# Three plain fp32 steps in the first half batch in place of eight, with a planner that counts table loads and transfer issue

## The chip, the cores and the metric

The kernel runs on one core of one Trainium2 chip. The metric is device time of one execution in microseconds (us). A core has five engines that run their own instruction streams in order: TensorE (PE in the profile; its weight loads are listed apart as PEld), VectorE (DVE), ScalarE (ACT), GpSimd (POOL) and SyncE (SP), which here issues all transfers. Inputs and outputs are fp32.

## The reference

Sliding-window attention with pooled keys and values, followed by a gated feed-forward layer, for 4 batches of 768 positions, 8 heads of 64, model width 512 and inner width 1024. Cut to what is computed:

```
block, window = 32, 16
k_sum = k in blocks of 32, max;  v_sum = v in blocks of 32, mean
scores = [ scale * q @ k^T where |i - j| < 16, else -1e9 ;  scale * q @ k_sum^T + log(32) ]
a = softmax(scores);  x = a @ [v ; v_sum]          # (B, 768, 512)
xk = mu_k * x + (1 - mu_k) * x_prev                # x_prev: x shifted by one position
xr = mu_r * x + (1 - mu_r) * x_prev
k = max(xk @ w_k, 0);  v = (k * k) @ w_v
r = 1 / (1 + exp(-(xr @ w_r)))
out = r * v
```

## The kernel before

A batch is cut into two halves of 384 positions; the eight halves are called by batch and half (b, hf). The attention of one half and one pair of heads is a *unit*: 24 small score products (L441), six masked copies with a running minimum on VectorE (L452), six exponentials on ScalarE (L456), sums and reciprocals on VectorE (L462, L463), six scalings on GpSimd (L468, tile `y`), two groups of three transposes on TensorE (L475, tile `pt`), their copies on ScalarE (L479), 24 value products (L488, tile `av`) and a copy of the result. A half has four units, so there are 32.

The feed-forward layer of a half begins with `mix` (L510 to L524), which forms xr and xk per pair of heads. From the second half on, each is then split into a high fp32r part (`cast` on ScalarE) and the low rest (`sub` on VectorE, L524). Three *gate tiles* give xr @ w_r, each followed by a sigmoid (L533) into a `z` tile. Then come eight *steps* j = 0 to 7: a *first product* xk @ w_k for 128 inner columns (L580), relu and square on ScalarE (L587, L589), a split of the square into `kh` and `kl` (L593 to L595), and a *second product* with w_v (L606) that accumulates over the eight steps into three PSUM tiles. After step 7, VectorE multiplies these with `z` (L636, the *results*), and they are stored. PSUM has four tiles called `mm` (mm_132 to mm_135 in the order's rows): the gates, the first products and the three accumulators share them.

A product is made in one of two ways. In the split way it takes three fp32r products, high by high, high by low and low by high: 12 matmuls in a first product, 9 in a second. In the plain way (`single`) it is one fp32 product with unsplit operands: 4 and 3 matmuls, each of which stands as two records in the trace. In half (0, 0), before the change, all eight steps and the gate are plain. The weights come as 64-bit words; ScalarE and VectorE turn each into fp32 (L307, L310, L312), and a split into high and low (L324 or L325, L327) follows for all 20 weight tiles, since every later half uses them.

The order of instructions on every engine comes from a planner. The program records operations with an engine, a due time and dependencies; `Plan.schedule` then assigns buffers and places each operation by the lengths in a table (`LENGTH`), and the instructions are emitted in that order, which the engines keep. Due times come from constants: `GATE0` and `GATE1` for the gates of the first two halves, `PERIOD` between later gates, `STEP0` and `STEP` between steps, `SECOND` between the units of half (0, 1). `warm` products (L660) on a tile of zeros are put where the planner sees TensorE idle, up to `WARM_END`. The planner lets SP start a transfer at most `EARLY` ns ahead of its due time and reckons 60 ns for its issue.

Of the kernel before, what the change touches and what calls it, by code (L numbers as in the profile page):

```python
# [20 lines left out]
P = 128  # L21
# [18 lines left out]
    score=900, transpose=340, vtrans=200, vpool=900, vsel=240, spread=560, spread_p=900, values=1000, gate=2790, gate32=930, e1=2090, e1_32=2800,  # L40
    e2a=1400, e2b=700, e2=700, e2_32=2800, e2l_32=930,
    warm=220, kred=860, kred2=470, kmax=190, kcopy=340, vred=860, mask=204, rc=310, evac=475, mixd=535, sub=475, khv=300,
    result=695, wbits=340, wor=612, wsub=612, tiny=60,
    exp=380, pts=380, vm=160, mixa=520, cast=405, relu=525, square=530, sigmoid=500, sigmoid3=4000, wscale=570, wcast=530,
    norm=345, wscale_p=640, wcast_p=640, mixa_p=860, kcopy_p=630, evac_a=375, fill=735,
# [7 lines left out]
STEP0 = 6800  # L53
GATE1 = 92000
PERIOD = 52000
STEP = 4800
# [44 lines left out]
class Plan:  # L101
# [36 lines left out]
    def schedule(self):  # L138
# [16 lines left out]
        dma = port = 0  # L155
# [10 lines left out]
        while any(ready.values()):  # L166
            best = None
            for e, now in engines.items():
# [3 lines left out]
                for o, at in ready[e]:  # L172
                    if o.name == "warm":
                        fill = max(now, at), o
                        continue
                    start, need, ok = max(at, now, o.due - EARLY if e == "SP" else 0), {}, True
                    for x in o.bufs:
# [14 lines left out]
                    key = (start if late else now, o.due, o.n)  # L192
# [9 lines left out]
            o.cost, o.emit = o.ways[e]  # L202
            for f in o.ways:
                ready[f] = [x for x in ready[f] if x[0] is not o]
# [32 lines left out]
def tile_kernel(ctx: ExitStack, tc: tile.TileContext, q, k, vT, v, mask, ident, pool, sel, mu, w_k, w_v, w_r, out):  # L237
# [266 lines left out]
    def mix(b, hf, which, p):  # L504
# [14 lines left out]
        if first:  # L519
            return xa  # L520
# [29 lines left out]
    def gate_parts(x, z):  # L550

        ps = [buf("mm") for _ in range(NTT)]
        for p in range(NPAIR):
            for t in range(NTT):
                op("PE", "gate32", GATE0 - (NPAIR - 1 - p) * FIRST + 930 * t, lambda p=p, t=t: nc.tensor.matmul(  # L555
                    ps[t].t, x[p].t[:, t * P:(t + 1) * P], w_f["wr", p].t, start=(p == 0), stop=(p == NPAIR - 1)),
                   reads=[(x[p], 0), (w_f["wr", p], 0), *([(ps[t], 0)] if p else [])], writes=[(ps[t], 0)])
# [224 lines left out]
```

## Time and profile before

| | |
|---|---|
| Median of 3 runs | 461.58 us (461.45 to 462.07) |
| Profiled execution | 462.56 us |
| Its span, first to last instruction | 460.8 us |
| Granted TensorE clock, mean | 0.999 |
| Busy: TensorE, ScalarE, VectorE, GpSimd | 449.6, 288.1, 254.7, 112.3 us |
| Table loads on ScalarE | 20 of 1.283 us |

The profiled execution took 1.76 us more than its span and 0.98 us more than the median of the runs. Stages of the span can be told by TensorE's instructions: the first plain first product of half (0, 0) starts at 41.95 us, the first gate tile of half (0, 1) at 95.37 us, that half's first product of step 0 at 112.66 us, and the last matmul ends at about 457 us. Busy time in the profile counts an engine as busy from an instruction's start to its end, overlaps once; instructions that follow each other closely overlap by up to 0.1 us, so a start-to-start distance is somewhat shorter than a mean duration.

### The profile page before, as it was taken

Reading aid. Unit: us, or ns where it says so; the run is one execution under the profiler, and the core shown is the slowest. Engines: PE = TensorE matmul, PEld = TensorE weight load, DVE = VectorE, ACT = ScalarE, POOL = GpSimd, SP = SyncE. Lnnn points to the kernel's source line nnn. Section 1 sums busy time; section 2 is a strip of 40 time slices with the busy share of each in tenths; the row PEclk is TensorE's granted clock in tenths of the full one; section 3 lists DMA queues with packets and bytes.
Section 4 is the critical chain, followed back from the end, with each engine's and each line's share of the span. In section 5 each row is a group of like instructions: output and inputs, shape, how many; then the busy total and the mean of one; then the engine's idle time right before and its main releaser. Section 6 shows DMA issues by size and latency. Waiting matters only on the chain.

```text
span 460.8 us, 9597 instructions
## 1 busy us (share of the span) xinstructions
PE 449.6 (98%) x3510; PEld 363.2 (79%) x3510; DVE 254.7 (55%) x846; ACT 288.1 (63%) x811; POOL 112.3 (24%) x238
## 2 busy tenths in 40 slices
PE   8999999988999999999999999999999999999996
PEld 8755655556788888987788888987788889988895
DVE  4789798963642566365444478357364455131213
ACT  3878989876875657258976558248977565232221
POOL 0762565622334002004343002104242201000000
PEclk9999999999999999999999999999999999999999
DMA  8963598652202067036002049017000010001001
GB/s 279 396 228 119 184 324 284 232 209 67 75 8 61 1 224 302 1 91 229 16 14 63 1 130 392 4 43 271 19 16 14 0 70 0 1 1 68 1 0 70
DMA packets 24230, 51.96 MB, mean 113 GB/s; under 512 B 2935, under 2 KB 10743, under 8 KB 24183
## 3 DMA queue, kind: packets, MB, share of 16 engines
q1 hardware_dynamic: 24183, 51.35, 32.5%
q8 instruction: 28, 0.46, 0.4%
q14 instruction: 19, 0.16, 0.1%
HBM read 43.28 MB, written 6.29 MB: 108 GB/s over the span
## 4 chain that ended last, share of the span: by engine, by line
PE 88%; ACT 7%; POOL 2%; SPq 1%; DVE 1%; issue 1%; DMA 0%; POOLq 0%; ACTq 0%
PE mm L606 29%; PE mm L580 28%; PE pt L475 5%; PE av L488 5%; PE sc L441 4%; PE mm L542 4%; PE mm L543 4%; PE mm L544 4%; ACT y L456 3%; PE mm L555 2%; PE pt L660 2%; POOL y L468 2%; ACT L456 1%; ACT pts L479 1%; PE mm L380 1%
## 5 line engine op out<-in xcount | busy, mean ns | idle before, releaser
L580 PE MATMUL mm<-xs,w 128*128 128x384 f32 x736 | 149.8, 352 | 0.0
L580 PEld LDWEIGHTS mm<-xs,w 128*128 128x128 f32 x736 | 130.4, 188 | 12.5 <-issue 1.4
L468 POOL TENSOR_SCALAR y<-y,rc 128x120 f32<-128x120 f32 x192 | 91.2, 493 | 167.5 <-DVE rc L463 138.7
L606 PE MATMUL mm<-w,kh 128*128 128x512 f32 x336 | 91.8, 402 | 0.0
L587 ACT ACTIVATE r<-mm 128x384 f32<-128x384 f32 x64 | 31.2, 487 | 91.9 <-PE mm L580 91.8
L456 ACT ACTIVATE y<-y,mn 128x120 f32<-128x120 f32 x192 | 73.5, 385 | 12.2 <-DVE mn L452 11.9
L606 PEld LDWEIGHTS mm<-w,kh 128*128 128x128 f32 x336 | 60.7, 188 | 11.2 <-issue 0.2
L593 DVE CAST kh<-r 128x384 fp32r<-128x384 f32 x44 | 16.1, 365 | 75.2 <-ACT r L589 75.1
L452 DVE CUSTOM_DVE_ANT_0 y<-sc,mask_sb 128x120 f32<-128x120 f32 x192 | 42.4, 277 | 25.1 <-PE sc L441 22.7
L606 PE MATMUL mm<-w,kl 128*128 128x512 f32 x168 | 52.3, 406 | 0.0
L524 DVE TENSOR_TENSOR xs<-xa,xs 128x384 fp32r<-128x384 f32 x56 | 30.1, 552 | 29.5 <-ACT xs L522 29.2
L479 ACT COPY pts<-pt 120x384 f32<-120x384 f32 x64 | 30.3, 474 | 14.8 <-PE pt L475 13.3
L516 DVE SCALAR_TENSOR_TENSOR xa<-vx,mu_sb,xa 128x384 f32<-128x384 f32 x56 | 33.7, 628 | 6.2 <-ACT xa L510 5.4
L456 ACT ACTIVATION_READ_ACCUMULATOR y<-y,mn 128x1 f32 x192 | 36.2, 189 | 0.0
L475 PE MATMUL pt<-ident_sb,y 128*120 128x128 f32 x192 | 32.7, 279 | 3.0 <-POOL y L468 2.5
L542 PE MATMUL mm<-w,xs 128*128 128x512 f32 x84 | 33.6, 399 | 2.0 <-ACT z L533 2.0
L606 PEld LDWEIGHTS mm<-w,kl 128*128 128x128 f32 x168 | 30.1, 188 | 6.1
L589 ACT ACTIVATE r<-r 128x384 f32<-128x384 f32 x64 | 33.6, 524 | 1.1
L488 PEld LDWEIGHTS av<-pts,vx 120*64 120x64 f32 x768 | 25.2, 137 | 11.4 <-issue 10.0
L475 PEld LDWEIGHTS pt<-ident_sb,y 128*120 128x120 f32 x192 | 22.3, 137 | 15.1 <-POOL y L468 6.4
L595 DVE TENSOR_TENSOR kl<-r,kh 128x384 fp32r<-128x384 f32 x56 | 31.8, 568 | 4.1 <-ACT kh L594 1.1
L544 PE MATMUL mm<-w,xs 128*128 128x512 f32 x84 | 32.8, 391 | 0.0
(66 smaller groups left out, 539.7 us busy)
## 6 DMA issues: line engine op xcount, KB each, us to landing
vx<-in_v SPq DMA_DIRECT2D x32, 384.0 KB
kt<-in_k SPq DMA_DIRECT2D x15, 544.0 KB
qt<-in_q SPq DMA_DIRECT2D x32, 192.0 KB
out<-z SPq DMA_DIRECT2D x24, 256.0 KB
st<-in_vT SPq DMA_DIRECT2D x12, 384.0 KB
st<-in_w_k SPq DMA_DIRECT2D x8, 512.0 KB
st<-in_w_v SPq DMA_DIRECT2D x8, 512.0 KB
st<-in_w_r SPq DMA_DIRECT2D x4, 512.0 KB
```

The costliest lines, as they stand in the source:

```text
L452: op("DVE", "mask", None, lambda h=h, i=i, var=var: nc.vector.tensor_tensor_reduce(out=y[h].t[:, i, :], in0=sc[h].t[:, i, 0:NK], in1=mask_ ...
L456: op("ACT", "exp", None, lambda h=h, i=i: nc.scalar.activation(y[h].t[:, i, :], y[h].t[:, i, :], AF.Exp, bias=mn[h].t[:, i:i + 1], scale=-1.0,
L468: op("POOL", "norm", None, lambda h=h, i=i: nc.gpsimd.tensor_scalar(out=y[h].t[:, i, :], in0=y[h].t[:, i, :], scalar1=rc.t[:, NSL * h + i: ...
L475: nc.tensor.transpose(out=pt[h].t[0:NK, i * P:(i + 1) * P], in_=y[h].t[:, i, :], identity=ident_sb)
L479: op("ACT", "pts", None, lambda h=h: nc.scalar.copy(out=pts[h].t, in_=pt[h].t[0:NK, 0:NSL * P].rearrange("p (i c) -> p i c", c=P)), reads= ...
L488: nc.tensor.matmul(av.t[hs, w * QW:(w + 1) * QW], windows(vw)[:, w, hs], pts[h].t[:, i, c * QW:(c + 1) * QW], start=True, stop=True,)
L516: op("DVE", "mixd", None, lambda: nc.vector.scalar_tensor_tensor(out=xa.t, in0=xt.t[:, 1 + lo:1 + lo + HT], scalar=mu_sb[:, which, p:p + 1 ...
L542: nc.tensor.matmul(ps.t, xh.t[:, ts], h, start=(p == 0), stop=False)
L544: nc.tensor.matmul(ps.t, xl.t[:, ts], h, start=False, stop=(p == NPAIR - 1))
L580: nc.tensor.matmul(ps.t[:, 0:HT], w.t[:, p * P:(p + 1) * P], (x[p] if single else x[p][s]).t, start=(n == 0), stop=(n == len(terms) * NPAI ...
L589: op("ACT", "square", None, lambda: nc.scalar.activation(r.t, r.t, AF.Square), reads=[(r, 0)], writes=[(r, 0)])
L606: nc.tensor.matmul(acc[t].t, a.t[:, t * P:(t + 1) * P], v.bitcast(F32) if single else v, start=start, stop=stop)
```

## The change

In half (0, 0) the steps 0 to 2 stay plain, and the steps 3 to 7 become split (`PLAIN = 3, 3`). For this the four xk tiles of the half keep their plain form and get high and low parts as well (`halves`), and the splits of the weights are recorded ahead of that half's steps. The planner now counts a table load of 1300 ns when ScalarE goes from exponentials to sigmoids or back, 450 ns for each issue on SP, at most eight transfers under way, and keeps two weight tiles free for unpacking before it splits another. Most lengths are set to other values, and so are the due times: the gate of half (0, 1) is due at 76000 instead of 92000 ns, and its four units have due times written out.

```diff
-    score=900, transpose=340, vtrans=200, vpool=900, vsel=240, spread=560, ...
+    score=865, transpose=350, vtrans=200, vpool=800, vsel=330, spread=540, ...
...
-STEP0 = 6800
-GATE1 = 92000
-PERIOD = 52000
-STEP = 4800
+STEP0 = 4000
+PLAIN = 3, 3
+GATE1 = 76000
+PERIOD = 50000
+STEP = 4600
...
-EARLY = 15000
+EARLY = 20000
+ISSUE = 450
+LANES = 8
+TABLE = 1300
+TABLES = dict(sigmoid=1, sigmoid3=1, exp=0, wscale=0)
...
-SECOND = 9000
-UNITS = 6000
+SECOND = 58000, 64000, 70000, 76000
+UNITS = 5500
...
+                    if o.name == "wcast" and len(free_slots["w"]) < owed + 2:
+                        continue
...
+                    if e == "SP":
+                        start = max(start, lanes[-LANES])
...
-                    key = (start if late else now, o.due, o.n)
+                    load = e == "ACT" and TABLES.get(o.name, table) != table
+                    key = (start if late else now, o.due + TABLE * load, o.n)
...
+            if e == "ACT" and TABLES.get(o.name, table) != table:
+                o.cost += TABLE
+                table = 1 - table
             o.start = start
             if e == "SP":
-                engines[e] = start + 60
+                engines[e] = start + ISSUE
                 dma = max(dma, start + 600) + o.size * DMA_NS_PER_BYTE
                 o.finish = dma + DMA_FIXED - 600
+                lanes.append(o.finish)
...
         if first:
-            return xa
+            return (xa,)
+        return halves(xa)
+
+    def halves(xa):
         xh, xl = buf("xs", F32R), buf("xs", F32R)
...
-        single = b + hf == 0
+        plain = PLAIN if b + hf == 0 else (0, 0)
         acc, ks = [], {}
 
         def first(j):
             ps, r = buf("mm"), buf("r")
-            kh, kl = ks[j] = (r, None) if single else (buf("kh", F32R), buf("kl", F32R))
+            single = j < plain[0]
+            kh, kl = ks[j] = (r, None) if j < plain[1] else (buf("kh", F32R), buf("kl", F32R))
...
     x = mixes(0, 0, 0)
+    if PLAIN[0] < NCV:
+        x = [(xa, *halves(xa)) for xa, in x]
     for p in range(NPAIR):
-        unit(0, p, 1, sets[p], gate_due(0, 1) - 9000 - (NPAIR - 1 - p) * SECOND)
-    experts(0, 0, x, z)
+        unit(0, p, 1, sets[p], SECOND[p])
     for i in range(NCK):
         split("wr", i)
     for j in range(NCV):
         split("wk", j)
         split("wv", j)
+    experts(0, 0, x, z)
```

The planner then makes another order of the whole program. Three places of it follow. The line numbers of the changed program are some 17 to 22 higher than those of the program before.

ScalarE around the three sigmoids of half (0, 1), before. `z<-mm` rows are the sigmoids, all three from mm_133; `y` rows are exponentials.

```order
L456 ACTIVATE y_92,sm_100<-y_92,mn_96 128x120 x3
L533 ACT_TABLE_LOAD
L533 ACTIVATE z_111<-mm_133 128x512
L501 COPY vx_74<-av_131 128x384
L479 COPY pts_105<-pt_130 120x384
L510 ACTIVATE xa_112<-vx_74,om_sb 128x384
L533 ACTIVATE z_0_1264<-mm_133 128x512
L479 COPY pts_106<-pt_130 120x384
L456 ACT_TABLE_LOAD
L456 ACTIVATE y_93,sm_101<-y_93,mn_97 128x120 x3
L456 ACTIVATE y_94,sm_101<-y_94,mn_98 128x120 x3
L522 CAST xs_0_771<-xa_112 128x384
```

The same place after the change.

```order
L473 ACTIVATE y_94,sm_101<-y_94,mn_98 128x120 x3
L542 CAST xs_0_700<-xa_113 128x384
L553 ACT_TABLE_LOAD
L553 ACTIVATE z_111<-mm_134 128x512
L542 CAST xs_0_719<-xa_114 128x384
L527 ACTIVATE xa_112<-vx_74,om_sb 128x384
L429 ACTIVATE vm_86<-pt_130 24x128
L553 ACTIVATE z_0_1396<-mm_135 128x512
L542 CAST xs_0_726<-xa_115 128x384
L542 CAST xs_1_1200<-xa_112 128x384
L496 COPY pts_107<-pt_130 120x384
L553 ACTIVATE z_0_1396<-mm_132 128x512
L608 ACTIVATE r_116<-mm_134 128x384
```

The exponentials of the last unit of half (0, 1) have moved ahead of the first sigmoid, the table is not loaded between the three sigmoids, and the three gate tiles lie in three PSUM tiles. In the whole program 18 table loads are left of 20.

VectorE around the first result of half (0, 0) (`z_108`), before: a reciprocal, a low part of the next half's xr, a sum of v for batch 1, and the result.

```order
L462 TENSOR_SCALAR sm_101<-sm_101 128x6
L463 RECIPROCAL rc_104<-sm_101 128x6
L524 TENSOR_TENSOR xs_0_776<-xa_112,xs_0_771 128x384
L392 TENSOR_REDUCE vs_84<-st_124 128x24
L636 TENSOR_TENSOR z_108<-mm_135,z_108 128x512
L452 ISA y_91,mn_95<-sc_128,mask_sb 128x120
```

After: the last low part of xr of half (0, 1) (`xs_1_1310`), the four second parts of its xk (`xa`), the first result, the last masks of the half's last unit, the second result, and the first low part of xk.

```order
L544 TENSOR_TENSOR xs_1_1310<-xa_115,xs_1_1285 128x384
L533 SCALAR_TENSOR_TENSOR xa_112<-vx_70,mu_sb,xa_112 128x384
L533 SCALAR_TENSOR_TENSOR xa_113<-vx_73,mu_sb,xa_113 128x384
L533 SCALAR_TENSOR_TENSOR xa_114<-vx_76,mu_sb,xa_114 128x384
L533 SCALAR_TENSOR_TENSOR xa_115<-vx_79,mu_sb,xa_115 128x384
L658 TENSOR_TENSOR z_108<-mm_135,z_108 128x512
L469 ISA y_94,mn_98<-sc_129,mask_sb 128x120
L469 ISA mn_98 128x1
```

The first result has moved ahead of the last masks of half (0, 1). On TensorE the order there is now: two parts of the last second product of half (0, 0), gate tile 0 into mm_134, gate tile 1 into mm_135, the third part, gate tile 2 into mm_132, and the first product of half (0, 1) into mm_134. Before, it was the three gate tiles, all into mm_133, then a first part of the second product, and the first product into mm_133.

SP's queue around the first keys of batch 1 (`kt_61<-in_k`), before.

```order
L306 DMA st_124<-in_w_k 128x1024
L424 DMA qt_66<-in_q 128x384
L306 DMA st_122<-in_w_v 128x1024
L306 DMA st_123<-in_w_k 128x1024
L306 DMA st_124<-in_w_v 128x1024
L306 DMA st_122<-in_w_k 128x1024
L424 DMA qt_67<-in_q 128x384
L342 DMA kt_61<-in_k 128x1088
```

After.

```order
L323 DMA st_124<-in_w_k 128x1024
L359 DMA kt_61<-in_k 128x1088
L441 DMA qt_66<-in_q 128x384
L323 DMA st_122<-in_w_v 128x1024
L323 DMA st_123<-in_w_k 128x1024
L441 DMA qt_67<-in_q 128x384
L441 DMA qt_64<-in_q 128x384
L323 DMA st_124<-in_w_v 128x1024
```

The keys of batch 1 have moved ahead of four weight loads and two loads of q.

More of the change, by code (lines that the diff above doesn't have):

```diff
@@ L39 @@
 LENGTH = dict(
[L40 to L45, printed above, removed]
+    score=865, transpose=350, vtrans=200, vpool=800, vsel=330, spread=540, spread_p=900, values=930, gate=2740, gate32=930, e1=2100,
+    e1_32=2690, e2a=1400, e2b=705, e2=705, e2_32=2600, e2l_32=930,
+    warm=223, kred=865, kred2=470, kmax=90, kcopy=280, vred=865, mask=204, rc=320, evac=470, mixd=535, sub=475, khv=280,
+    result=600, wbits=340, wor=610, wsub=605, tiny=60,
+    exp=380, pts=375, vm=160, mixa=515, cast=405, relu=380, square=425, sigmoid=500, sigmoid3=1600, wscale=570, wcast=530,
+    norm=345, wcast_p=640, mixa_p=600, kcopy_p=450, evac_a=375,
 )
@@ L154, in schedule @@
         ready = {e: [] for e in engines}
-        dma = port = 0
+        dma = port = table = 0
+        lanes = [0] * LANES
+        owed = sum(o.name == "wor" for o in self.ops)
         order = []
@@ L202, in schedule @@
             o.cost, o.emit = o.ways[e]
+            owed += dict(wor=-1, wcast=1, wsub=-1).get(o.name, 0)
             for f in o.ways:
@@ L555, in gate_parts @@
                 op("PE", "gate32", GATE0 - (NPAIR - 1 - p) * FIRST + 930 * t, lambda p=p, t=t: nc.tensor.matmul(
-                    ps[t].t, x[p].t[:, t * P:(t + 1) * P], w_f["wr", p].t, start=(p == 0), stop=(p == NPAIR - 1)),
-                   reads=[(x[p], 0), (w_f["wr", p], 0), *([(ps[t], 0)] if p else [])], writes=[(ps[t], 0)])
+                    ps[t].t, x[p][0].t[:, t * P:(t + 1) * P], w_f["wr", p].t, start=(p == 0), stop=(p == NPAIR - 1)),
+                   reads=[(x[p][0], 0), (w_f["wr", p], 0), *([(ps[t], 0)] if p else [])], writes=[(ps[t], 0)])
         def sigmoids():
@@ L579, in products @@
                     for p in range(NPAIR):
-                        nc.tensor.matmul(ps.t[:, 0:HT], w.t[:, p * P:(p + 1) * P], (x[p] if single else x[p][s]).t,
+                        nc.tensor.matmul(ps.t[:, 0:HT], w.t[:, p * P:(p + 1) * P], x[p][s].t,
                                          start=(n == 0), stop=(n == len(terms) * NPAIR - 1))
@@ L584, in first @@
             op("PE", "e1_32" if single else "e1", e1_due(b, hf, j), products,
-               reads=[(a, 0) for a in x] + [(w_f["wk", j], 0)] if single else
-               [(a, 0) for pair in x for a in pair] + [(w["wk", j], 0) for w in (w_h, w_l)], writes=[(ps, 0)])
+               reads=list(dict.fromkeys([(pair[s], 0) for pair in x for _, s in terms] + [(w, 0) for w, _ in terms])),
+               writes=[(ps, 0)])
             op("ACT", "relu", None, lambda: nc.scalar.activation(r.t, ps.t[:, 0:HT], AF.Relu),
@@ L590, in first @@
                reads=[(r, 0)], writes=[(r, 0)])
-            if single:
+            if kl is None:
                 return
@@ L600, in second @@
             kh, kl = ks[j]
+            single = kl is None
             due = e2_due(b, hf, j)
```

4 lines of the change are left out of this document (2 added, 2 removed).

## The prediction

> **What bounds the kernel now.** I read the page first: what is busy, and the chain that ended last.
>
> ```profile
> span 460.8 us, 9597 instructions
> PE 449.6 (98%) x3510; PEld 363.2 (79%) x3510; DVE 254.7 (55%) x846; ACT 288.1 (63%) x811; POOL 112.3 (24%) x238
> PE 88%; ACT 7%; POOL 2%; SPq 1%; DVE 1%; issue 1%; DMA 0%; POOLq 0%; ACTq 0%
> ```
>
> TensorE is idle for 11.2 us of the whole span and carries 88% of the chain. Next, the busy time in stages. Columns are TensorE, its weight loads, VectorE, ScalarE, GpSimd, granted clock, transfers.
>
> ```profile
> 0.00:42.00 42.00, 39.53 (x457) 28.41 (x458) 31.86 (x118) 28.40 (x91) 16.07 (x37) 1.00 0.73 264
> 42.00:95.40 53.40, 53.40 (x393) 30.85 (x391) 47.83 (x151) 48.52 (x142) 30.75 (x47) 1.00 0.75 252
> 95.40:112.70 17.30, 13.63 (x123) 9.99 (x121) 8.20 (x33) 12.76 (x34) 5.49 (x15) 1.00 0.32 116
> 112.70:170.00 57.30, 57.30 (x486) 47.88 (x485) 28.63 (x99) 36.41 (x105) 12.93 (x28) 1.00 0.20 62
> 371.20:457.00 85.80, 85.80 (x418) 75.65 (x416) 29.73 (x60) 28.36 (x56) 1.32 (x1) 1.00 0.05 19
> 457.00:460.80 3.80, 0.01 (x1) 0.00 (x0) 0.73 (x2) 0.00 (x0) 0.00 (x0) 0.82 0.55 207
> ```
>
> The idle time lies in the start (2.47 us), the gate stage of half (0, 1) (3.67) and the tail (3.79); 1.3 us is left for everything between 112.7 and 457. From 42 to 95.4 us TensorE is never idle, but VectorE and ScalarE are about 90% busy too, and after 112.7 us they are not. So the second stage has three nearly full engines, and all later ones have one. TensorE's rows in time give the ends of the stages and the waits in the third.
>
> ```profile
> 41.95 2.74 PE L580 MATMUL mm<-xs,w 128*128 128x384 f32 x8
> 101.65 0.50 PE L542 MATMUL mm<-w,xs 128*128 128x512 f32 x1 [1.98 <-ACT z L533]
> 112.39 0.51 PE L475 MATMUL pt<-ident_sb,y 128*120 128x128 f32 x3 [1.69 <-POOL y L468]
> 112.66 2.36 PE L580 MATMUL mm<-xs,w 128*128 128x384 f32 x12
> ```
>
> Two waits make up the 3.67 us: gate tile 1 waits for the sigmoid that empties the one PSUM tile, and a transpose waits for GpSimd's scalings. I cost the change from 41.95 to 112.66 us, the first product of half (0, 1): 70.71 us.
>
> **TensorE's own work.** The chain of waits has each product at its bare length.
>
> ```profile
> 50.47 2.58 PE mm L606 x6
> 60.82 2.58 PE mm L580 x8
> 157.66 2.10 PE mm L606 x9
> 144.12 2.11 PE mm L580 x12
> 45.40 1.38 PE L660 MATMUL pt<-zero_sb 128*128 128x128 f32 x10
> 46.95 0.61 PE L660 MATMUL pt<-zero_sb 128*128 128x128 f32 x4
> ```
>
> A plain product takes 2.58 us, a split one 2.11 (first) or 2.10 (second). Five first products save 5 x 0.47 = 2.35 us, five second ones 5 x 0.48 = 2.40: 4.75 in all. The order adds a shift. Before, two of the three parts of the last second product (0.86 us each, 1.72 together) stood behind the first product of half (0, 1); now all three stand ahead of it. So inside the stage second products fall from 7 x 2.58 + 0.86 = 18.92 to 3 x 2.58 + 5 x 2.10 = 18.24, and the stage loses 2.35 + 0.68 = 3.03 us, while 1.72 us leave what follows. Seven warm products stood in the stage (14 records; 1.38 + 0.61 less some overlap, 1.7 us); the order after has none there. If TensorE never waited, the stage would end at 112.66 - 3.67 - 1.7 - 3.03 = 104.3 us.
>
> **VectorE.** That end isn't free: the low parts must be made in time. Before, from the first mask of half (0, 1) (40.6 us) until the last low part of its xk (98.7 us):
>
> ```profile
> 40.60:98.70 58.10, 58.10 (x421) 34.01 (x421) 51.22 (x170) 50.78 (x149) 31.71 (x49) 1.00 0.74 253
> L524 DVE TENSOR_TENSOR xs<-xa,xs 128x384 fp32r<-128x384 f32 x56 | 30.1, 552 | 29.5 <-ACT xs L522 29.2
> L593 DVE CAST kh<-r 128x384 fp32r<-128x384 f32 x44 | 16.1, 365 | 75.2 <-ACT r L589 75.1
> L452 DVE CUSTOM_DVE_ANT_0 y<-sc,mask_sb 128x120 f32<-128x120 f32 x192 | 42.4, 277 | 25.1 <-PE sc L441 22.7 <-PE pt L475 2.2
> L636 DVE TENSOR_TENSOR z<-mm,z 128x512 f32<-128x512 f32 x24 | 16.0, 685 | 3.9 <-PE mm L606 3.9
> L327 DVE TENSOR_TENSOR w<-w,w 128x512 fp32r<-128x512 f32 x19 | 12.8, 691 | 0.8 <-POOL w L325 0.8
> L310 DVE TENSOR_SCALAR we<-st 128x512 uint32<-128x512 uint32 x20 | 9.4, 468 | 0.2
> L312 DVE SCALAR_TENSOR_TENSOR w<-wc,we 128x512 uint32<-128x512 uint32 x19 | 13.6, 715 | 1.7 <-ACT wc L307 0.8
> ```
>
> VectorE was busy for 51.2 us and idle for 6.9. In the order after, the step that decides is the first result of half (0, 0): gate tile 1 goes into the PSUM tile that this result empties, and it stands behind the four second parts of xk. Counted from the same first mask to the end of that result, the order has 6 low parts more (3.3 us; `sub` of xk and of the squares), 3 `kh` (1.1), 4 masks (1.0), one split of a weight (0.7), the result itself (0.7) and four short ones (about 0.9, an estimate by the mask's row), and less by two `we` (0.9) and one `wor` (0.7): +6.1 us, 57.3 in all. The result ends at 40.6 + 57.3 = 97.9 us if VectorE never waits, and at 104.8 if it waits as long as before. Behind it TensorE does gate tile 1, the third part, gate tile 2 and short transposes: two gates of 12 matmuls at 2.10 / 9 us each (2.8), 0.7 and 0.3, together 6.6. The first product of half (0, 1) then starts between 104.5 and 111.4 us.
>
> **ScalarE** has the same stage from the table load ahead of the first sigmoids (43.3 us) to the relu after that first product (115.05):
>
> ```profile
> 43.30:115.00 71.70, 68.03 (x522) 42.33 (x521) 54.87 (x181) 60.46 (x169) 36.08 (x62) 1.00 0.64 217
> L456 ACT ACTIVATE y<-y,mn 128x120 f32<-128x120 f32 x192 | 73.5, 385 | 12.2 <-DVE mn L452 11.9
> L324 ACT CAST w<-w 128x512 fp32r<-128x512 f32 x10 | 6.1, 614 | 1.3 <-DVE w L312 1.3
> 99.71 1.28 ACT L533 ACT_TABLE_LOAD   x1
> 101.00 0.60 ACT L533 ACTIVATE z<-mm 128x512 f32<-128x512 f32 x1
> ```
>
> The order gives it net ten instructions more (casts of the half's xk, of weights and of squares, five exponentials earlier, fewer scalings for `mix`), between 0.39 and 0.61 us each, so 3.9 to 6.1, and two table loads less (2.6): +1.3 to +3.5. It was idle for 11.2 us. Without idle time the relu starts at 105.1 to 107.3, the first product 2.4 us earlier, at 102.7 to 104.9; with all of it, at 113.9 to 116.1.
>
> A load takes 1.28 us in the trace, and the sigmoid starts 0.01 us behind it. [...]
>
> **The rest.** In the start, before 42 us, VectorE gets one weight tile's unpacking more and one copy less (+0.6 us) and was idle for 10 of 42 us, ScalarE for 13.6; both cover it, and without that cover it would cost the 0.6. I take 0. After the first product of half (0, 1), the products are the same, so the sequence keeps its length but for the 1.72 us; its 1.3 us of idle time is all that a better order could gain. The tail doesn't change. On SP the keys of batch 1 pass four weight loads and two loads of q. One transfer of about half a megabyte then lands ahead of four others of that size; the row of L312 shows VectorE waiting 0.8 us in all for what ScalarE makes of the weights, so there is time to spare and I cost it at nothing. Without that cover a late transfer stops VectorE's queue, which is the last rival below.
>
> **The sum.** I take the middle for VectorE's idle time, 108.0 us for the first product: the waits for exponentials and casts are still in the order, but some of its new instructions (the low parts of half (0, 0)'s own xk, a weight's split) have operands ready well ahead and can fill them. Both ends stay for the range. That is 112.66 - 108.0 = 4.7 us, and with 1.7 behind it 6.4. The profiled execution took 462.56 us, 1.76 above its span and 0.98 above the median; 456.2 for it, and 455.2 us against the median of 461.58.
>
> **Rivals.**
>
> *Only the matmuls count.* The new lengths and due times pack nothing better, and the warm products' time turns to waiting. Then the 4.75 us of products are the gain: 456.8. For it: TensorE's waits were only 3.67 us in that stage, and each could be replaced by another. Against it: the order puts the gates into three PSUM tiles, so that the 1.98 us wait is gone as it stood.
>
> *GpSimd and VectorE hold each other up.* Six scalings of a unit take 3.0 us in one place and 5.0 in another.
>
> ```profile
> 44.40 3.02 POOL L468 TENSOR_SCALAR y<-y,rc 128x120 f32<-128x120 f32 x6 [0.42 <-DVE rc L463]
> 54.67 5.02 POOL L468 TENSOR_SCALAR y<-y,rc 128x120 f32<-128x120 f32 x6 [2.33 <-DVE rc L463]
> ```
>
> Beside the second, VectorE unpacks and splits weights. Nine more low parts (0.55 us) come into the stage; if each holds up the scalings by its whole length, and transposes wait for all of it, that is 5.0 us: the first product at 113.0, 0.4 us later than before, 1.4 us gained, 460.2. The wait of 1.69 us above is of this kind; but most scalings have slack of a whole unit. [...]
>
> *ScalarE keeps all its idle time.* First product at 113.9 to 116.1, a change of -0.5 to +1.7, 461.1 to 463.3 us.
>
> *Slower: VectorE waits for keys.* Four key reductions of batch 1 now stand ahead of the first result, the first of them right behind the first masks, and VectorE's queue stops at each.
>
> ```profile
> DVE kg L356 <- DMA kt<-in_k: 9.9, 7, 3.4
> ```
>
> Such waits cost 9.9 us in seven places, 3.4 at the longest. Four of the longest make 13.6 on top of 104.5: first product at 118.1, +3.7 us, 465.3. It decides from waits of 10.8 us on (the first product behind 115.3, 0.9 us slower). Against it: SP issues these keys earlier too.
>
> **How the numbers follow.** About 0.2% (0.9 us) is what a measurement of this kernel can tell from no change. Chances: the forecast 0.57, only the matmuls 0.17, ports 0.10, ScalarE 0.07, keys 0.09. The first three are faster (0.84); ScalarE's case is split between same and slower. The low end is VectorE without idle time: 104.5, so 8.2 + 1.7 = 9.9 us, and the 1.3 of the later stages: 450.4. The high end takes in the ports, 460.2. Beyond it lie ScalarE and the keys, 0.16; I leave 0.03 below.
>
> **What would show it.** Right, if the first plain product starts within 0.6 us of 41.95, the first product of half (0, 1) at 104 to 111 us, gate tile 1 waits for VectorE's `z` row, 18 table loads are left, and from that first product to the last matmul's end the time is about 342.6 us. Wrong, if VectorE shows long waits on `in_k`, if TensorE waits for `kl` or for weights between the split steps 3 to 7, or if that later distance changes by over 1.5 us.

## The result, and the profile after

The changed kernel took 450.4 us in the median of 4 runs (449.13 to 451.05); the kernel before, run beside it, 461.82 (461.45 to 464.41, 4 runs). The ratio is 0.9738, with a 95% interval of 0.9696 to 0.9779. The forecast was 455.2: the sign was right, the gain nearly twice as large, and the time lies on the low end of the range. The profiled execution took 450.6 us. From its page, the span, the engines' busy time and the chain that ended last:

```profile
span 448.8 us, 9629 instructions
PE 441.7 (98%) x3521; PEld 366.3 (82%) x3521; DVE 261.2 (58%) x866; ACT 282.9 (63%) x808; POOL 104.8 (23%) x237
PE 90%; ACT 3%; DMA 3%; DVE 2%; SPq 1%; issue 0%; DVEq 0%
```

ScalarE's part of the chain fell from 7% to 3%, and TensorE is idle for 7.1 us of the span where it was 11.2. The busy time by stages, in the columns of before (TensorE, weight loads, VectorE, ScalarE, GpSimd, granted clock, transfers):

```profile
41.56:94.85 53.29, 52.42 (x494) 38.02 (x493) 51.65 (x185) 51.80 (x163) 28.02 (x50) 1.00 0.74 257
94.85:104.28 9.43, 9.43 (x48) 7.56 (x44) 8.01 (x19) 7.14 (x20) 4.90 (x11) 1.00 0.44 149
104.28:159.58 55.30, 55.30 (x482) 47.09 (x480) 32.05 (x106) 36.37 (x105) 11.69 (x28) 1.00 0.26 80
445.04:448.80 3.76, 0.00 (x0) 0.00 (x0) 0.71 (x2) 0.00 (x0) 0.00 (x0) 1.00 0.56 209
41.20:97.60 56.40, 55.53 (x507) 40.32 (x505) 54.76 (x193) 54.06 (x169) 30.72 (x54) 1.00 0.73 254
```

The gate stage has shrunk from 17.30 to 9.43 us and holds no idle time of TensorE. In the last row, which runs from the first mask of half (0, 1) to the end of the first result, TensorE, VectorE and ScalarE are busy for 55.53, 54.76 and 54.06 of 56.40 us: three engines at 96 to 98%. TensorE's rows in time, at the points of before:

```profile
41.56 2.74 PE L601 MATMUL mm<-xs,w 128*128 128x384 f32 x8
97.71 0.43 PE L562 MATMUL mm<-w,xs 128*128 128x512 f32 x1
104.03 0.49 PE L492 MATMUL pt<-ident_sb,y 128*120 128x128 f32 x3
104.28 2.33 PE L601 MATMUL mm<-xs,w 128*128 128x384 f32 x12
```

Gate tile 1 (97.71) and the transposes ahead of the first product carry no wait any more; before they had 1.98 and 1.69 us. The first product of half (0, 1) came at 104.28 instead of 112.66. Where the 11.95 us up to the last matmul's end lie, against the forecast for the same pieces:

| piece of TensorE's time | before | after | change | forecast |
|---|---|---|---|---|
| start of the first plain product | 41.95 | 41.56 | -0.39 | 0 |
| to the first product of half (0, 1) | 70.71 | 62.72 | -7.99 | -4.66 |
| to that of half (1, 0) | 57.21 | 55.30 | -1.91 | -1.72 |
| to that of half (2, 0) | 105.81 | 104.68 | -1.13 | 0 |
| to that of half (3, 0) | 105.76 | 104.71 | -1.05 | 0 |
| to the last matmul's end | 75.55 | 76.07 | +0.52 | 0 |
| sum | | | -11.95 | -6.38 |

The 0.39 us at the start is no gain of the change: in other runs whose order ahead of it is that of the changed kernel, the first plain product starts anywhere between 40.70 and 42.06 us. The two sums differ by 5.6 us and the medians by 4.8, since the profiled execution of before lay 0.98 us above its median and that of after 0.2. Table loads fell from 20 to 18:

```profile
L473 ACT ACT_TABLE_LOAD x9 | 11.5, 1283 | 0.9 <-PEq L795 0.7
L553 ACT ACT_TABLE_LOAD x8 | 10.3, 1283 | 0.1
L581 ACT ACT_TABLE_LOAD x1 | 1.3, 1283 | 0.0
```

### The profile page after: what moved, and what is told of

Read it like the earlier page. It is cut to its first block, busy times and chain, and to the rows that moved or that the text cites. A ratio compares the mean times of both kernels' runs of the same rounds, so it can differ in the third digit from the quotient of the medians.

```text
span 448.8 us, 9629 instructions
## 1 busy us (share of the span) xinstructions
PE 441.7 (98%) x3521; PEld 366.3 (82%) x3521; DVE 261.2 (58%) x866; ACT 282.9 (63%) x808; POOL 104.8 (23%) x237
## 4 chain that ended last, share of the span: by engine, by line
PE 90%; ACT 3%; DMA 3%; DVE 2%; SPq 1%; issue 0%; DVEq 0%
PE mm L628 30%; PE mm L601 29%; PE av L505 5%; PE pt L492 5%; PE sc L458 4%; PE mm L562 4%; PE mm L564 4%; PE mm L563 4%; DMA vx<-in_v 3%; PE mm L575 2%; ACT y L473 1%; PE pt L412 0%; DVE z L658 0%; ACT pts L496 0%; PE mm L397 0%
## 5 line engine op out<-in xcount | busy, mean ns | idle before, releaser
L601 PE MATMUL mm<-xs,w 128*128 128x384 f32 x756 | 147.4, 343 | 0.0
L601 PEld LDWEIGHTS mm<-xs,w 128*128 128x128 f32 x756 | 132.9, 188 | 7.4 <-issue 0.7
L485 POOL TENSOR_SCALAR y<-y,rc 128x120 f32<-128x120 f32 x192 | 83.9, 455 | 142.1 <-DVE rc L480 117.1
L628 PE MATMUL mm<-w,kh 128*128 128x512 f32 x366 | 100.3, 402 | 0.2 <-ACT kh L615 0.2
L628 PEld LDWEIGHTS mm<-w,kh 128*128 128x128 f32 x366 | 66.1, 188 | 12.6 <-ACT kh L615 0.5
L614 DVE CAST kh<-r 128x384 fp32r<-128x384 f32 x55 | 21.1, 384 | 92.6 <-ACT r L610 83.6
L628 PE MATMUL mm<-w,kl 128*128 128x512 f32 x183 | 57.0, 406 | 0.0
L628 PEld LDWEIGHTS mm<-w,kl 128*128 128x128 f32 x183 | 32.9, 188 | 7.4 <-issue 0.5
L616 DVE TENSOR_TENSOR kl<-r,kh 128x384 fp32r<-128x384 f32 x61 | 34.7, 569 | 4.2 <-ACT kh L615 0.7
L562 PE MATMUL mm<-w,xs 128*128 128x512 f32 x84 | 33.3, 397 | 0.0
L564 PE MATMUL mm<-w,xs 128*128 128x512 f32 x84 | 32.9, 392 | 0.0
L563 PE MATMUL mm<-w,xs 128*128 128x512 f32 x84 | 32.8, 390 | 0.0
```

Of the source, the lines that this page charges most:

```text
L485: op("POOL", "norm", None, lambda h=h, i=i: nc.gpsimd.tensor_scalar(out=y[h].t[:, i, :], in0=y[h].t[:, i, :], scalar1=rc.t[:, NSL * h + i: ...
L562: nc.tensor.matmul(ps.t, xh.t[:, ts], h, start=(p == 0), stop=False)
L563: nc.tensor.matmul(ps.t, xh.t[:, ts], l, start=False, stop=False)
L564: nc.tensor.matmul(ps.t, xl.t[:, ts], h, start=False, stop=(p == NPAIR - 1))
L601: nc.tensor.matmul(ps.t[:, 0:HT], w.t[:, p * P:(p + 1) * P], x[p][s].t, start=(n == 0), stop=(n == len(terms) * NPAIR - 1))
L616: op("DVE", "sub", None, lambda: nc.vector.tensor_tensor(out=kl.t, in0=r.t, in1=kh.t.bitcast(F32), op=ALU.subtract), reads=[(r, 0), (kh, 0 ...
```

## The experiments

All ratios are against runs of the kernel before on the same chip, with 95% intervals.

### What the plain steps and the planner each bring

The changed kernel with all eight steps plain again:

```diff
-PLAIN = 3, 3
+PLAIN = 8, 8
```

> The changed planner, lengths and due times, with all eight steps of half (0, 0) plain as before. Theory A (the planner's order took away VectorE's idle time and the gate stage's waits, and the split products give their own 4.75 us beside that): about 4.75 us slower than the changed kernel, 455 us, so some 6.5 us faster than before. Theory B (the gain comes from the split products, which free TensorE in the crowded stage; the planner's numbers matter little): near 460 us.

Measured: 453.67 us (453.05 to 454.12), ratio 0.9833 [0.9818, 0.9847]. TensorE's first product of half (0, 1) in time, and then the busy time in as long a stretch as above, from the first mask of half (0, 1) on (the first result starts only at 98.6 us here):

```profile
108.16 2.33 PE L601 MATMUL mm<-xs,w 128*128 128x384 f32 x12
```

```profile
40.00:96.40 56.40, 55.62 (x415) 32.35 (x414) 49.37 (x174) 52.63 (x158) 27.71 (x51) 1.00 0.77 256
```

The new planner without the plain steps' change takes off 7.6 us by the medians. VectorE is busy for 49.4 of 56.4 us there; with the split steps it was 54.8. The split steps add 3.3 us by the medians. In the traces they shorten the way from the first plain product to the first product of half (0, 1) by 5.1 us (67.79 to 62.72), a little more than the 4.75 that the matmuls are worth; 1.2 us less shows at the end because the first plain product came at 40.37 us with eight plain steps and at 41.56 with three, a difference no larger than the scatter of the start, and 0.7 because what follows took longer.

The other half, the three plain steps under the old planner. The diff is against the changed kernel; the table of lengths and all constants of due times are the old ones too, and transfers under way have no limit:

```diff
 PLAIN = 3, 3
...
-ISSUE = 450
+ISSUE = 60
...
-TABLES = dict(sigmoid=1, sigmoid3=1, exp=0, wscale=0)
+TABLES = {}
...
```

> Three plain steps, but the old planner: old lengths, old due times, no table loads counted, 60 ns per issue, no limit on transfers, transfers at most 15000 ns early. Theory A: the products' 4.75 us at most, 457 us or more, with VectorE idle for some 6 us again between the first mask of half (0, 1) and the first result. Theory B: nearly the whole gain, 450 to 452 us.

Measured: 463.62 us (463.5 to 464.77), ratio 1.0055 [1.004, 1.007]: slower, though the products take 4.75 us less. In the profiled execution, the slowest of the four by 1.1 us, the first product came 4.3 us later than before, there are 22 table loads instead of 20, and the wait for the one PSUM tile is still there; the granted clock fell behind it (0.98 in the mean of the last row below; seven matmuls of gate tile 1 take 0.63 us each, its last 0.39). TensorE's busy time also counts warm products, and this order has 7.15 us of them up to the first product, where the kernel before has 1.99 and the changed kernel none (the product in time, the wait, and the warm products alone from the first plain product on):

```profile
116.92 2.35 PE L601 MATMUL mm<-xs,w 128*128 128x384 f32 x12
```

```profile
PE mm L562 <- ACT z L553: 1.7, 1, 1.7
```

```profile
42.04:116.92 74.88, 7.15 (x52) 6.43 (x52) 0.98 0.64 212
```

So less work on TensorE alone bought nothing in this stage. Whether the warm products held TensorE up or filled time in which it would have waited, no run shows. The larger part of the gain is the order's, and the split steps pay only together with it.

### Is VectorE a bound, too

The changed kernel in its own order, with 13 low parts between the first mask of half (0, 1) and the first result computed twice, which gives VectorE 6.1 us more:

```diff
+    vector = [o for o in order if o.eng == "DVE"]
+    names = [o.name for o in vector]
+    lo = [n for n, x in enumerate(names) if x == "mask"][24]
+    hi = names.index("result")
+    twice = {o.n for o in vector[lo:hi] if o.name in ("sub",)}
...
         o.emit()
+        if o.n in twice:
+            o.emit()
```

> The changed kernel in exactly its order, with the 13 low parts that VectorE makes between the first mask of half (0, 1) and the first result computed twice: 13 x 0.47 = 6.1 us more on VectorE, output unchanged. If VectorE sets the end of that stage (it was busy for 54.8 of 56.4 us): 5 to 6 us slower, about 456 us. If TensorE alone sets it and VectorE runs ahead: less than 2 us slower.

Measured: 456.17 us (455.57 to 458.21), ratio 0.9896 [0.9871, 0.9921], 5.8 us above the changed kernel. TensorE's two longest waits for VectorE up to its first product of half (0, 1), and that product in time:

```profile
PE mm L562 <- DVE z L658: 1.6, 1, 1.6
PE mm L628 <- DVE kl L616: 0.9, 1, 0.9
```

```profile
110.23 2.33 PE L601 MATMUL mm<-xs,w 128*128 128x384 f32 x12
```

Nearly the whole addition reached the end: from the first plain product on TensorE is idle for 5.2 us, 0.9 in the changed kernel. The wait of gate tile 1 for VectorE's `z`, which the prediction named, appears as soon as VectorE is fuller. In the changed kernel TensorE and VectorE thus end together, with a few tenths of a microsecond between them.

### Was VectorE's idle time of before room, or a part of its order

The kernel before, in its own order, with 14 low parts of weights (0.6 us each) in the same stretch computed twice: 8.4 us for an engine that was idle for 6.9.

```diff
...
+    hi = [n for n, x in enumerate(names) if x == "sub"][7] + 1
+    twice = {o.n for o in vector[lo:hi] if o.name in ("wsub",)}
...
```

> The kernel before, in its own order; 14 low parts of weights (each a subtraction of about 0.60 us on VectorE) between the first mask of half (0,1) and the last low part of its xk are computed twice: 14 x 0.60 = 8.4 us more work on VectorE in the stage in which it was idle for 6.9 us. Theory A (the idle time was room that other waits left, and could be filled): 461.8 to 464.8 us, under 3 us slower, and the stage's idle time on VectorE shrinks towards 1 us. Theory B (the idle time belongs to the order, work is added behind it, as the prediction took half of it to stay): 468 to 471 us, with 5 us or more of the idle time still there.

Measured: 470.97 us (470.65 to 471.24), ratio 1.0203 [1.0186, 1.022]: 9.1 us slower. The busy time up to the last low part of xk, with the added work, and TensorE's row at gate tile 1:

```profile
41.95:105.80 63.85, 60.39 (x431) 35.03 (x429) 60.06 (x176) 50.13 (x149) 32.82 (x49) 0.97 0.71 231
```

```profile
108.18 0.79 PE L542 MATMUL mm<-w,xs 128*128 128x512 f32 x1 [3.37 <-ACT z L533]
```

Of the 6.9 us of idle time 3.8 are left, so that some 3 were filled, which lies between the two theories; the time fits the second. The first product of half (0, 1) came at 120.73 us, 8.1 later. TensorE's idle time up to it grew from 3.67 to 7.54 us, with the wait at gate tile 1 growing from 1.98 to 3.37, and the granted clock fell twice: its mean is 0.97 over the 63.85 us of the row above and 0.70 over the 5.64 us from gate tile 1 on (108.18 to 113.82), which costs about 1.9 and 1.7 us, an estimate from these means. The loss is therefore not all VectorE's. In a fixed order the idle time was room for less than half of its length. The prediction reasoned on this as if the old waits would come along with the new order, half of them; the new order has its own waits.

### What the three PSUM tiles are worth

A first attempt gave the three gate tiles one place without sorting the emission again.

```diff
+    gates = sorted((o for o in order if o.name == "gate"), key=lambda o: o.n)[:3]
+    tiles_of = [next(x for x in o.bufs if x.pool == "mm") for o in gates]
+    for x in tiles_of[1:]:
+        x.place = tiles_of[0].place
```

> The changed kernel in exactly its order, but the three gate tiles of half (0, 1) share one PSUM tile, as before the change. If the three PSUM tiles are what took the wait of gate tile 1 away: gate tile 1 waits for the first sigmoid, which ended at 101.0 us while the tile started at 97.7, so 3 to 5 us slower, about 454 us. If the order alone did it: within 1 us of the changed kernel.

Measured: 452.04 us (451.25 to 452.21), ratio 0.9793 [0.9776, 0.9809]. It tells nothing of the question: gate tile 1 was emitted ahead of the first sigmoid, which then reads a tile that is overwritten, so the wait that was to be measured didn't arise. The second attempt emits the chain gate, sigmoid, gate, sigmoid, gate, sigmoid, first product in this order, and leaves each engine's order as it was (`share_one` sorts the emission by these and all other dependencies):

```diff
...
+        chain = [gates[0], sigmas[0], gates[1], sigmas[1], gates[2], sigmas[2], following]
...
+        for a, b in zip(chain, chain[1:]):
+            need[b.n].add(a.n)
...
+    order = share_one(order)
...
```

> The changed kernel, each engine's order unchanged, but the three tiles of the gate sum of half (0,1) lie in one PSUM tile, so that gate tile 1 waits for the first sigmoid, gate tile 2 for the second, and the first product of half (0,1) for the third. If the three PSUM tiles are worth what the waits of before were (1.7 us and 2.0 us): 453.0 to 455.5 us, first product of half (0,1) 3 to 5 us later than 104.28. Rival (other TensorE work that stands between takes the time, or VectorE is what sets the product): 450 to 451.5 us.

Measured: 457.34 us (456.53 to 460.36), ratio 0.9918 [0.9891, 0.9946], 6.9 us above the changed kernel and more than either theory gave. The first matmuls of gate tile 1 and of the first product, and two stretches of time around tile 1:

```profile
101.08 0.79 PE L562 MATMUL mm<-w,xs 128*128 128x512 f32 x1 [3.66 <-ACT z L553]
111.99 2.38 PE L601 MATMUL mm<-xs,w 128*128 128x384 f32 x12 [1.07 <-ACT z L553]
```

```profile
101.08:106.37 5.29, 5.29 (x12) 3.94 (x13) 0.00 (x0) 0.87 (x2) 0.68 (x3) 0.50 0.00 0
107.57:110.43 2.86, 2.86 (x12) 2.30 (x13) 2.23 (x6) 0.86 (x2) 0.00 (x0) 1.00 0.49 125
```

Two waits make 4.7 us. Behind the longer one the granted clock is 0.50, and the 12 matmuls of tile 1 take 5.29 us; those of tile 2, at the full clock, 2.86. That is 2.4 us on top, 7.2 in all, against a first product that came 7.7 us later. What the three tiles save in this order is the waits and the clock that the longer one costs.

### Which part of the planner's change does it

Each part was put back by itself in the changed kernel: the old lengths; the old due times (`STEP0`, `GATE1`, `PERIOD`, `STEP`, `SECOND`, `UNITS`); no count of table loads; no count of transfer issue. The planner's fifth change, the two weight tiles that it keeps free, stands in every run of the changed program, and no run takes it out.

```diff
-    score=865, transpose=350, ..., relu=380, square=425, sigmoid=500, sigmoid3=1600, ...
+    score=900, transpose=340, ..., relu=525, square=530, sigmoid=500, sigmoid3=4000, ...
```

> The changed kernel with the old table of lengths, everything else new. Theory L (wrong lengths made VectorE's idle time: an order whose lengths are off stops its in-order queues): loses most of the planner's 7.6 us (all-plain run against before), 455 us or more. Theory D (the due times did it, the lengths matter little): within 1.5 us of 450.4.

```diff
-GATE1 = 76000
+GATE1 = 92000
...
-SECOND = 58000, 64000, 70000, 76000
+SECOND = 56000, 65000, 74000, 83000
...
```

> The changed kernel with the old due times (GATE1, PERIOD, STEP0, STEP, SECOND by its old formula, UNITS), everything else new. Theory D: 455 us or more. Theory L: within 1.5 us of 450.4.

```diff
-TABLES = dict(sigmoid=1, sigmoid3=1, exp=0, wscale=0)
+TABLES = {}
```

> The changed kernel without the count of table loads (no cost, no preference), everything else new. If the count is what removed two loads and the wait at the gates: 20 or more loads again and 2.6 us or more slower, 453 us or more. If lengths or due times did it: within 1 us of 450.4.

```diff
-EARLY = 20000
-ISSUE = 450
+EARLY = 15000
+ISSUE = 60
...
-                        start = max(start, lanes[-LANES])
+                        pass
```

> The changed kernel with 60 ns per issue on SP, no limit on transfers under way, and transfers at most 15000 ns early; everything else new. VectorE waited only 1.1 us for keys in the changed kernel, so both theories: within 1 us of 450.4; over 2 us slower only if early keys are what keeps VectorE's queue going.

| put back | time, us | ratio to before | above the changed kernel | first product of half (0, 1) | warm products in the stretch up to it, us | table loads | half (1, 0) to (2, 0) |
|---|---|---|---|---|---|---|---|
| nothing | 450.4 | 0.9738 [0.9696, 0.9779] | | 104.28 | 0 | 18 | 104.68 |
| old lengths | 460.91 (459.53 to 462.86) | 0.9987 [0.9973, 1.0002] | 10.5 | 115.22 | 10.57 | 28 | 104.66 |
| old due times | 455.75 (455.59 to 455.96) | 0.9869 [0.9854, 0.9884] | 5.3 | 110.61 | 5.37 | 22 | 104.74 |
| no count of table loads | 458.85 (458.19 to 459.25) | 0.9934 [0.992, 0.9949] | 8.5 | 109.49 | 0 | 20 | 105.92 |
| no count of issue | 450.2 (450.02 to 451.38) | 0.9754 [0.9739, 0.9769] | -0.2 | 104.42 | 0.71 | 18 | 104.72 |

Of the four parts, three cost time when they are put back. Their losses sum to 24 us, twice the gain: they aren't additive, since each setting makes the planner lay out another order, and with one order for each setting, what a part is worth can't be told from how good the order happens to be. The count of transfer issue buys nothing here: the order is another, the time the same.

The losses don't stand in the same place. With the old lengths TensorE has 10.57 us of warm products in the 73.58 us from the first plain product to the first product of half (0, 1) (these products alone):

```profile
41.64:115.22 73.58, 10.57 (x76) 9.17 (x76) 1.00 0.65 211
```

Without them that stretch would be 63.0 us long, and it is 62.72 in the changed kernel. So the loss stands where the planner, by its own lengths, reckoned TensorE idle and put warm products; whether TensorE would have had to wait there anyway, no run shows. Without the count of table loads there are none, and TensorE is idle for 4.08 us of its stretch instead of 0.87.

The last column is the second finding: the batches behind the first lose the 1.1 us that they had gained when table loads aren't counted, and only then. That has a run of its own: the changed program with the old lengths, due times and issue and eight plain steps, and of the new settings this one alone. The two weight tiles kept free stand in it too; with the count off, its planner lays out nearly the order of before (the cast of one weight moves from GpSimd to ScalarE, and two pairs on VectorE change places), and that order was not timed. Against the same settings without the count:

```diff
-TABLES = {}
+TABLES = dict(sigmoid=1, sigmoid3=1, exp=0, wscale=0)
```

> The kernel before with one change: its planner counts the table loads of ScalarE (old lengths, old due times, old transfer issue, eight plain steps). Theory (the count takes time off the later stages, and shortens the first one only together with the right lengths and due times): the three later stages of a batch's length 104.7 us in place of 105.8, so 458 to 460.5 us. Rival (nothing without the other changes, or a loss, as the plain steps alone had): 461.0 to 465 us.

Measured: 457.77 us (457.56 to 458.08), ratio 0.9914 [0.9897, 0.993], better than expected. The busy time from the first product of half (1, 0) to that of (2, 0), in this run, after and before, and TensorE's waits there in before (after and this run have none):

```profile
167.17:271.97 104.80, 104.80 (x845) 89.42 (x844) 58.30 (x202) 68.37 (x195) 23.28 (x57) 1.00 0.32 107
```

```profile
159.58:264.26 104.68, 104.68 (x845) 89.38 (x844) 58.48 (x204) 67.43 (x193) 22.47 (x58) 1.00 0.33 111
```

```profile
169.87:275.68 105.81, 105.16 (x846) 89.51 (x844) 57.81 (x201) 69.67 (x198) 23.14 (x55) 1.00 0.30 99
```

```profile
PE pt L475 <- POOL y L468: 0.4, 1, 0.4
PE pt L475 <- ACT pts L479: 0.2, 1, 0.2
```

Of the 1.13 us, 0.65 was idle time of TensorE, two waits of transposes; the other 0.5 is busy time that is spread over several groups (transposes 8.2 to 8.0 us, value products 7.5 to 7.3, first products 36.8 to 36.5), and its cause stays open. All three orders have six table loads in this stretch, so it isn't fewer loads. The two waits are gone with the count and stand again, 0.4 and 0.2 us, in the changed kernel without it. That the planner now knows that ScalarE is away for 1.3 us at each load, so that the transposes' operands come in time, fits this and isn't shown beyond it. By itself the count is worth 3.9 us by the medians and 4.7 in the traces: 1.9 at the first product (110.80), 0.8 in the stage behind it and 2.0 in the two long ones.

### Which of the lengths

In the old table the sigmoid over three banks stands with 4000 ns, in the new one with 1600.

```diff
-    ..., sigmoid=500, sigmoid3=1600, ...
+    ..., sigmoid=500, sigmoid3=4000, ...
```

> The changed kernel, with one recorded length put back for the planner: the sigmoid over three banks 4000 ns, as in the table before, in place of 1600. If this length is what costs the kernel with all old lengths its 10.5 us (its gate came late in the planner's clock): 457 to 461 us, the third first product of half (0,0) near 66 us in place of 50.3. Rival (the loss is from the many other lengths together): 450 to 453 us.

And the other way about, all old lengths but this one:

```diff
-    score=865, transpose=350, ..., relu=380, square=425, sigmoid=500, sigmoid3=1600, ...
+    score=900, transpose=340, ..., relu=525, square=530, sigmoid=500, sigmoid3=1600, ...
```

> The changed kernel with all the old recorded lengths but one: the sigmoid over three banks keeps the new 1600 ns. If the long sigmoid's share (4.3 us, by the run with it alone) and that of the others add up: 455.5 to 457.5 us. Rival (the others carry the whole loss, or the parts do not add up): 459 us or more, or under 453 us.

Measured: 454.77 us (452.67 to 456.44), ratio 0.9847 [0.9807, 0.9888], and 459.1 us (457.98 to 459.87), ratio 0.9941 [0.9922, 0.996]. The long sigmoid costs some 4.4 us, less than expected, and the others 8.7 without it, against 10.5 for all: no one length carries it, and again the parts don't add up. The third first product of half (0, 0), which starts at 50.27 us in the changed kernel, came at 66.79 with all old lengths and at 64.22 with all but the sigmoid, but at 52.91 with the long sigmoid alone; so most of the delay there is the other lengths' doing. In the first of the two kernels the executions lie in two groups, 453 and 456.4 us, with a mean granted clock of 0.995 in the two of the slower group and 1.000 and 0.999 in the others. The profiled one, of the slower group, shows a pause of TensorE, and the granted clock behind it in the next 5 us (third number from the end):

```profile
94.01 0.49 PE L682 MATMUL pt<-zero_sb 128*128 128x128 f32 x2 [2.45 <-ACT pts L496]
```

```profile
95.00:100.00 5.00, 5.00 (x28) 4.03 (x25) 4.30 (x16) 4.44 (x16) 1.31 (x6) 0.66 0.34 103
```

### Two and four plain steps

```diff
-PLAIN = 3, 3
+PLAIN = 2, 2
```

> The changed kernel with two plain steps of each product in place of three. TensorE saves another 0.47 + 0.48 = 0.95 us, and VectorE gets two more splits (about 0.46 us and 0.6 us). If VectorE and TensorE both bind the stage, as the run with 6.1 us more on VectorE says: 450 to 452 us, nothing gained. Rival (TensorE alone binds): 449.3 to 449.7 us.

```diff
-PLAIN = 3, 3
+PLAIN = 4, 4
```

> The changed kernel with four plain steps of each product in place of three. TensorE has 0.47 + 0.48 = 0.95 us more in the stage, VectorE about 1 us less. If three plain steps are where the two engines are about even: 450.3 to 451.7 us, since TensorE has no idle time in the stage to hide it in. Rival (VectorE still sets the product): 449 to 450 us, a gain. Third case (the planner finds a worse order): above 452 us.

Measured: 451.66 us (451.31 to 452.48), ratio 0.9785 [0.977, 0.98] with two, 454.07 (453.72 to 456.67), ratio 0.9846 [0.9816, 0.9875] with four. With two steps the products take 0.95 us less and the kernel 1.3 us more. That is not a test of two bounds: the planner made another order, with 2.46 us of warm products ahead of the first product where the changed kernel has none. Four came out 3.7 us worse, which is more than their 0.95 us: the planner made 24 table loads, again another order. Neither run therefore says anything on the balance, and no experiment here beats the changed kernel by more than the 0.2 us of the run without the count of issue.

## Why the prediction was right and wrong

**Right: what the products save and that it isn't enough.** TensorE's floor for the stage, 104.3 us if it never waited, was met at 104.28. That the two agree to 0.02 us is luck: there were 0.87 us of waits, the start came 0.39 us earlier, and the work took 0.5 us less than reckoned. The shift of 1.72 us behind the first product is there (-1.91). The tail is 3.76 us for 3.80. The first plain product lies 0.39 us from 41.95, inside the 0.6, and the order's 18 table loads are there.

**Right in kind: VectorE sets the end too.** With 6.1 us more on it the kernel loses 5.8. From gate tile 1 to the first product it took 6.57 us, by the sum 6.6. The named wait, gate tile 1 behind VectorE's `z`, does not stand in the trace of after: the result ends at 97.58 us, 0.13 before the tile starts, and only the tile's weight load waited for it, 0.2 us behind other products. It stands in the kernel with more on VectorE.

**Wrong: the step that put 108.0 us for the first product.** It failed in two terms of VectorE's sum, forecast to end the result at 40.6 + 57.3 + 3.45 = 101.35 us; it ended at 97.58.

- The work was put at 51.2 + 6.1 = 57.3 us, and was 54.76. The added work was rightly counted: the busy times of the groups in that stretch, each group by itself, sum to 60.0 us before and 66.4 after, 6.4 more. But neighbours overlap, and the 51.2 to which the durations were added is a time that counts overlaps once. Here are two low parts with a weight's split between, and masks:

```profile
89.49 0.55 DVE L544 TENSOR_TENSOR xs<-xa,xs 128x384 fp32r<-128x384 f32 x1
89.96 0.68 DVE L344 TENSOR_TENSOR w<-wc,w 128x512 fp32r<-128x512 f32 x1
90.56 0.55 DVE L544 TENSOR_TENSOR xs<-xa,xs 128x384 fp32r<-128x384 f32 x1
97.50 0.27 DVE L469 CUSTOM_DVE_ANT_0 y<-sc,mask_sb 128x120 f32<-128x120 f32 x1
97.70 0.08 DVE L469 DVE_READ_ACCUMULATOR2_ANT mn<- 128x1 f32 x1
97.70 0.27 DVE L469 CUSTOM_DVE_ANT_0 y<-sc,mask_sb 128x120 f32<-128x120 f32 x1
```

  A low part of 0.55 us occupies 0.47 until the next starts, a mask of 0.27 with its read of 0.08 occupies 0.20. Priced by the distances between starts that closely following instructions have in the trace of before, the two queues come to 47.3 and 52.2 us, +4.9, an estimate. Measured is +3.5: the rest is that the work that both orders have took up less time in the fuller queue (a `we` 0.43 us before and 0.39 after, since fewer of them stand ahead of a pause). That term was 2.5 us too large.

- The idle time was taken as half of the 6.9 us, 3.45, and was 1.64. One wait above 1 us is left in the stretch, for keys, and what cost most before, the sums' wait for exponentials, fell from 31.8 us in the whole run to 6.1 (the waits of the whole run, us in total, times and the longest, of before, then of after, and the one row in time):

```profile
DVE sm L462 <- ACT y L456: 31.8, 19, 2.3
```

```profile
DVE sm L479 <- ACT y L473: 6.1, 7, 1.5
DVE kg L373 <- DMA kt<-in_k: 7.4, 5, 3.4
```

```profile
68.43 0.95 DVE L373 TENSOR_REDUCE kg<-kt 128x48 f32<-128x768 f32 x1 [1.12 <-DMA kt<-in_k]
```

  That term was 1.8 us too large. With the first mask 0.58 us later than before, 2.54 + 1.81 - 0.58 = 3.77 us, which is 101.35 less 97.58. With both terms right VectorE gives 104.2 for the first product and TensorE 104.3, and there is no middle to choose.

**Wrong: "its 1.3 us of idle time is all that a better order could gain", and none of it in the forecast.** The time from the first product to the last matmul's end fell to 340.76 us, where 342.6 was forecast; the bound of 1.5 us that the prediction set itself is exceeded. The idle time was rightly sized (0.65 in each of the two long stages) and all of it went; 0.9 us of busy time of TensorE went with it, and 0.5 came back in the last stage. The run with the count of table loads alone, and the one without it, show that the count brings this; 0.5 us of the busy time in each long stage stays without a cause.

**The rivals.** *Only the matmuls count* (456.8): no; the matmuls without the order give 463.62, the order without the matmuls 453.67. *GpSimd and VectorE* ("ports" in the prediction's chances and range): no run shows any ports; the 192 scalings of the whole run took 83.9 us after and 91.2 before, so they are held up no more than before. *ScalarE keeps its idle time*: it was busy for 54.06 of 56.40 us. *Keys*: 7.4 us of waits in the whole run, 9.9 before, and one in this stage. *Slower*: the old planner with the three plain steps is slower by 0.55%, though not for the reason given; VectorE waits for keys once in that stage, for 1.5 us.

## What to carry to other kernels

Price an engine's queue by the distance between starts, old work and new alike, and don't add durations to a busy time that counts overlaps once: in a full queue the two differ by a sixth (60.0 and 51.2 us in the stage before), and a forecast whose end hangs on that engine moves by microseconds. Idle time belongs largely to an order; when a planner makes another one, take its idle time neither along nor in half, but work out which waits the new order still has, above all whether an engine that is away for a table load is now known to be. Look for filling work, too: the warm products count as busy time, and some of the slower orders here have 5 to 11 us of them. And cutting one engine's work alone, without an order made for it, can lose, as it did here by 0.55%.

## What the runs showed of the hardware

Behind some pauses of TensorE the granted clock fell to 0.50, and such a pause cost most of its own length again (2.4 us for one of 3.66, 1.7 for one of 2.04). The means of 0.50 over 5.29 us behind the pause of 3.66 us and of 0.66 over 5.00 us behind that of 2.45 us above are of this kind. In the profiled execution without the count of table loads a pause of 2.04 us was enough (the product behind it takes 4.44 us, its like 2.74), and the clock is 0.50 for 3.42 us, with 1.00 on both sides. First its matmul, then the busy time in three stretches, in the first of which TensorE is idle for 2.04 us:

```profile
48.53 4.44 PE L628 MATMUL mm<-w,r 128*128 128x512 f32 x6 [2.04 <-ACT r L610]
```

```profile
46.22:49.63 3.41, 1.37 (x4) 0.62 (x4) 0.90 (x3) 3.40 (x15) 0.76 (x1) 1.00 0.63 236
49.63:53.05 3.42, 3.42 (x6) 1.36 (x5) 3.42 (x8) 3.42 (x9) 3.21 (x4) 0.50 0.44 139
53.05:56.46 3.41, 3.41 (x33) 1.91 (x32) 3.17 (x6) 2.82 (x6) 3.32 (x4) 1.00 0.89 312
```

The pause of 1.98 us in the kernel before cost nothing: the clock is 1.00 around it and behind it, where gate tile 1 stands.

```profile
99.60:101.65 2.05, 0.07 (x1) 0.00 (x0) 1.00 (x5) 2.02 (x4) 1.21 (x4) 1.00 0.08 31
101.65:105.74 4.09, 4.09 (x39) 3.17 (x39) 0.62 (x1) 2.19 (x6) 0.96 (x3) 1.00 0.00 0
```

A shorter one did cost: in the run of the three plain steps under the old planner, gate tile 1 has 1.74 us of idle time ahead of it, and the transposes 3 us earlier 0.78; the tile's third matmul takes 0.63 us, its last 0.39.

```profile
105.47 0.51 PE L492 MATMUL pt<-ident_sb,y 128*120 128x128 f32 x3 [0.78 <-ACT vm L429]
108.42 0.50 PE L562 MATMUL mm<-w,xs 128*128 128x512 f32 x1 [1.74 <-ACT z L553]
109.09 0.63 PE L564 MATMUL mm<-w,xs 128*128 128x512 f32 x1
112.65 0.39 PE L564 MATMUL mm<-w,xs 128*128 128x512 f32 x1
```

So the length of the last pause alone doesn't tell whether the clock falls behind it; what does, no run here shows. The halved clock is also why pauses are worth more than their length in the sums: 6.1 us for the one of 3.66, which is its length and the 2.4 us that tile 1 took longer.
